# One group of six row turns after the value products, in a score buffer, copied by ScalarE

## Chip, cores and metric

The kernel runs on one core of a Trainium2 chip. The metric is the device time of one execution in microseconds. TensorE (PE in the profile, with its weight loads as PEld), VectorE (DVE), ScalarE (ACT), GpSimd (POOL) and SyncE (SP, which issues most DMAs) each run their own instructions in order and wait for each other by semaphores.

## What is computed

Sigmoid attention over 4 batches and 12 heads of 448 tokens, then a routed layer of 8 experts on the 1,792 tokens, then a dense layer with an ELU curve:

```python
def _attn_ref(q, k, v):
    scores = scale * np.matmul(q, k.transpose(0, 1, 3, 2)) - np.log(S)
    attn = 1.0 / (1.0 + np.exp(-scores))
    return np.matmul(attn, v)
...
x = attn_out.transpose(0, 2, 1, 3).reshape(B * S, H * D)   # 1792 x 768
x = _moe_ref(x=x, **moe_kwargs)     # skip score, argmax over 8 experts, two products, gate
return _moe2_ref(x=x, **moe2_kwargs)  # x @ w_in, ELU, @ w_out
```

## The kernel before

The attention loop runs over 24 steps (`steps`), one for each pair of heads of each batch, six pairs (`hp`) to a batch (`b`), and one more round for the last products. In step n, TensorE makes four groups of scores (`scores`, line 228, six matmuls over two banks each, out of a pool `pss` of three two-bank PSUM buffers), ScalarE turns each group into attention weights with one sigmoid (line 235), and TensorE then makes the sixteen value products of the step before (`mix`, line 242) into the one buffer `po`, which VectorE copies into `xT` (line 250). `xT` holds the attention output with its 768 features on the partitions.

The next stage wants x by token rows in DRAM (`x_d`). So 9 of the 14 tiles of 128 tokens (`LATE`) are turned inside the loop, one in each step with `hp > 1` whose batches lie far enough back. A turned tile is six TensorE transposes (`flip`, line 138), a copy from PSUM into `xr` (line 272) and a store by SyncE (line 274). In the kernel before, `rows` is a generator of two halves. The first half is three transposes behind the score groups and ahead of the value products, into the only buffer of pool `psx`, copied by VectorE; the second half is three transposes behind the value products, into the same buffer, copied by ScalarE. The other five tiles are turned after the loop, two halves each, in buffers of `pss`, and ScalarE makes all ten copies.

Beside this, each step splits half of the next q and k into two parts (`split_qk`: a ScalarE cast on line 220, then a VectorE subtraction on line 221), and VectorE converts 64-bit weights of the last layer by pieces (`narrow`, lines 146 to 166), up to two pieces after each of four points in the step. TensorE, ScalarE and VectorE run in the order of the program text (`manual_schedule`); SyncE's and GpSimd's orders are set by the scheduler. Buffers in a pool go round: a new tile of a tag waits until the readers of the tile that had the buffer are done.

After the loop come the routing of tokens (a chain of small VectorE operations), a gather of rows of `x_d` by GpSimd (line 706), the experts and the dense layer.

Of the kernel before, what the change touches and what calls it, by code (L numbers as in the profile page):

```python
# [12 lines left out]
F32 = mybir.dt.float32  # L13
# [10 lines left out]
P = 128  # L24
B, H, S, D = 4, 12, 448, 64
# [6 lines left out]
KD = DM // P  # L32
# [9 lines left out]
N2 = DM // 2  # L42
# [4 lines left out]
LATE = 9  # L47
# [42 lines left out]
def build(nc, tc, a):  # L90
# [3 lines left out]
    with ExitStack() as top:  # L94
# [42 lines left out]
        def flip(dst, src):  # L137
            nc.tensor.transpose(dst, src, ident)  # L138

        def wide_load(w, i, part=slice(None)):  # L140
            nc.sync.dma_start(w, wide[i].rearrange("p (n t) -> p n t", t=2)[:, part])
# [30 lines left out]
        with ExitStack() as st:  # L172
# [7 lines left out]
            pss = st.enter_context(tc.tile_pool(name="pss", bufs=3, space=PSUM))  # L180
            ps1 = st.enter_context(tc.tile_pool(name="ps1", bufs=1, space=PSUM))
            psx = st.enter_context(tc.tile_pool(name="psx", bufs=1, space=PSUM))
# [17 lines left out]
            xT = xp.tile([P, NP, NT], F32, name="xT")  # L200
            lgT = xp.tile([P, NT], F32, name="lgT")

            def load(b, t, first=False):
                qr = qkp.tile([P, 2, S], F32, name="qr")
                kr = qkp.tile([P, 2, S], F32, name="kr")
                if first:
                    for p in range(2):
                        nc.sync.dma_start(qr[:, p], q[b, t, :, p])
                        (nc.scalar, nc.sync)[p].dma_start(kr[:, p], k[b, t, :, p])
                    return qr, kr  # L210
                nc.sync.dma_start(qr, q[b, t])
                nc.sync.dma_start(kr, k[b, t])
                return qr, kr

            def split_tiles(raw):
                return raw, [qkp.tile([P, 2, S], F32R, name=n) for n in ("qh", "ql", "kh", "kl")]

            def split_qk(which, raw, parts, p=slice(None)):
                r, (hi, lo) = raw[which], parts[2 * which : 2 * which + 2]
                nc.scalar.copy(hi[:, p], r[:, p])  # L220
                nc.vector.tensor_sub(lo[:, p], r[:, p], hi[:, p])

            def scores(at, c, p, qh, ql, kh, kl):
                ps = pss.tile([P, 2, 512], F32, name="ps")
                for i, (kk, qq) in enumerate(((kh, qh), (kh, ql), (kl, qh))):
                    for j in range(2):
                        head = slice(64 * j, 64 * j + 64)
                        nc.tensor.matmul(  # L228
                            ps[:CP, j, :S],
                            kk[head, p, c * CP : (c + 1) * CP],  # L230
                            qq[head, p],
                            start=(i == 0),
                            stop=(i == 2),
                        )
                nc.scalar.activation(  # L235
                    at[:, :, c, :], ps[:CP, :, :S], AF.Sigmoid, bias=bias[:CP], scale=QK_SCALE
                )
# [25 lines left out]
                    )  # L263
                nc.vector.tensor_copy(lgT[:, b * S : (b + 1) * S], lg[:, :S])

            def rows(t, engines, pool=psx, tag="px"):
                xr = rowp.tile([P, DM], F32, name="xr")
                for g in range(2):
                    px = pool.tile([P, 512], F32, name="px", tag=tag)
                    for i in range(3):  # L270
                        flip(px[:, i * P : (i + 1) * P], xT[:, 3 * g + i, t * P : (t + 1) * P])
                    engines[g](xr[:, g * N2 : (g + 1) * N2], px[:, :N2])
                    yield
                nc.sync.dma_start(x_d[t * P : (t + 1) * P, :], xr)

            lgt = xp.tile([P, NTT, E + 1], F32, name="lgt")
# [12 lines left out]
            def run(gen):  # L289
                for _ in gen or ():  # L290
                    pass
# [111 lines left out]
            def load_v(n):  # L403
                vts[n] = qkp.tile([CP, 4, NCH, D], F32, name="vt", bufs=2)
                nc.sync.dma_start(vts[n], v[n // 3, :, 4 * (n % 3) : 4 * (n % 3) + 4])
# [24 lines left out]
            wide_load(wides[0], 0)  # L430
            done_rows = 0
            done_lgt = 0
            row = None
            prev = None
            nxt = None
            for n in range(steps + 1):
                b, hp = divmod(n, NP)
                T, p = divmod(n, 2)
                if p == 0 and n < steps:
                    if n:  # L440
                        cur = nxt
                    if T + 1 < steps // 2:
                        nxt = split_tiles(nxt_raw)
                        if T + 2 < steps // 2:
                            nxt_raw = load(*divmod(T + 2, 3))
                    else:
                        nxt = None
                if p == 1 and T + 1 < steps // 2:
                    load_v(T + 1)
                at = atp.tile([CP, 2, NCH, S], F32, name="at") if n < steps else None  # L450
                po = ps1.tile([P, 512], F32, name="po", tag="po") if n else None
                if m3 is not None and c0 + 1 < n:
                    nc.scalar.copy(wi0[0], m3)
                    nc.vector.tensor_sub(wi0[1], m3, wi0[0])
                    m3 = None
                if conv is None and narrowed < n * 2 * FA // (steps - 1):
                    mf = wi1 if narrowed == 2 else cvp.tile([P, DM], F32, name="mf")
                    w = wides[narrowed % 2]
                    if narrowed + 1 < 2 * FA:
                        wide_load(wides[(narrowed + 1) % 2], narrowed + 1)  # L460
                    sg = cvp.tile([P, DM], I32, name="sg", bufs=1)
                    mg = cvp.tile([P, DM], I32, name="mg", bufs=1)
                    conv = narrow(mf, w, sg, mg, False)
                if row is None and done_rows < LATE and hp > 1 and (done_rows + 1) * P <= b * S:
                    row = rows(done_rows, (nc.vector.tensor_copy, nc.scalar.copy))
                    done_rows += 1
                for c in range(NCH):
                    for c2 in range(NCH):
                        if c == 0 and n < steps:
                            scores(at, c2, p, *cur[1])  # L470
                        if c == 2 and n:
                            mix(c2, n - 1, *prev, po)
                    if nxt and n < steps and c == 1:
                        split_qk(p, *nxt)
                    if row is not None and c in (1, 3):
                        next(row, None)
                    if hp == 1 and b > 0 and c == 0:
                        logits(b - 1)
                    if hp == 1 and b > 0 and c in (2, 3):
                        m = min(4, b * S // P - done_lgt)  # L480
                        if m > 0 and b < B:
                            token_logits(done_lgt, m)
                            done_lgt += m
                    if n > SOON_STEP:
                        next(soon, None)
                    if n > SOON_STEP + 2:
                        next(soon, None)
                    for _ in range(2):
                        if conv is not None and next(conv, 1):
                            if narrowed == 0:  # L490
                                m3, c0 = mf.rearrange("p (c f) -> p c f", c=KD), n
                            elif narrowed != 2:
                                nc.sync.dma_start((wi_d, wo_d)[narrowed % 2][narrowed // 2], mf)
                            narrowed += 1
                            conv = None
                if row is not None:
                    run(row)
                    row = None
                prev = (vts.get(T), at)
            run(soon)  # L500
            logits(B - 1)
# [1 line left out]
            rowp = st.enter_context(  # L503
                tc.tile_pool(name="rowq", bufs=NTT - done_rows, reuse_waits="tile")
            )
            tail_rows = (nc.scalar.copy, nc.scalar.copy)
            run(rows(done_rows, tail_rows, pss, "ps"))
            token_logits(done_lgt, NTT - done_lgt)
            for t in range(done_rows + 1, done_rows + 3):
                run(rows(t, tail_rows, pss, "ps"))  # L510


            choose(SOON, NTT)
# [2 lines left out]
                nc.tensor.matmul(cnt, ones_b, p[:, 0, :E], start=(k_ == 0), stop=(k_ == 1))  # L516
            pos = positions(SOON, NTT, ps1, "po")
            for t in range(done_rows + 3, NTT):
                run(rows(t, tail_rows, pss, "ps"))
            rp = st.enter_context(tc.tile_pool(name="rp", reuse_waits="tile", bufs=1))  # L520

            def rt(shape, name, dt=F32):
# [62 lines left out]
            for k_, p in enumerate(counted):  # L585
                nc.tensor.matmul(
                    ordered, ones_b, p, start=(k_ == 0), stop=(k_ == len(counted) - 1)
# [548 lines left out]
        with ExitStack() as st:  # L1136
# [156 lines left out]
            for s, (bi, f) in enumerate(steps):  # L1293
# [12 lines left out]
                g = curve(nt * P, ph)  # L1306
                if bi + 1 < len(blocks):
                    u0, un = blocks[bi + 1]
                    turn, half = divmod(f - 6, 2)
                    if half == 0 and 0 <= turn < un:  # L1310
                        rows_next = rows_of(u0 + turn)
                    turn, half = divmod(f - 7, 2)
# [47 lines left out]
```

## Time and profile before

| what | us |
|---|---|
| three runs | 937.42, 937.55, 939.18 (median 937.55) |
| the profiled execution | 937.65 |
| its span, first to last instruction | 935.8 |
| TensorE busy in the span | 900.0 (96%) |
| VectorE, ScalarE, GpSimd busy | 560.1, 483.3, 69.0 |
| mean granted TensorE clock | 0.992 |
| attention loop | about 7 to 176 us of the span |

The profiled execution is read as follows. The chain that ended last tells which engine sets the pace at each time; the waits tell for whom an engine stood still; the timeline gives each instruction's start and length. The 1.85 us between span and time lie outside the instructions. A busy TensorE is not one at its peak: matmuls are pipelined, and their ends overlap the next one's start.

### The profile page before, as it was taken

How to read it: one execution, taken by the hardware profiler on the slowest of the kernel's cores; microseconds unless marked ns; L12 is line 12 of the kernel's file. 1: busy time of each engine (PE TensorE's matmuls, PEld its weight loads, DVE VectorE, ACT ScalarE, POOL GpSimd, SP SyncE). 2: the span in 40 equal slices, each digit the busy share in tenths (PEclk: the TensorE clock that was granted, in tenths of full speed). 3: DMA queues.
4: the chain of work that ended last, by engine and by line, in shares of the span. 5: the costliest groups of instructions: out<-in, count | busy, mean ns of one | idle time of the engine just before them, and what ended most of it. 6: DMA issues, size and time to landing. Idle time of an engine off the chain costs nothing.

```text
span 935.8 us, 13725 instructions
## 1 busy us (share of the span) xinstructions
PE 900.0 (96%) x5239; PEld 722.0 (77%) x5239; DVE 560.1 (60%) x871; ACT 483.3 (52%) x681; POOL 69.0 (7%) x69
## 2 busy tenths in 40 slices
PE   9999999899999998898899999999999999999998
PEld 4444444479997997788788888888888888888997
DVE  2776676867564664688488887533443434434664
ACT  7766676443354554576355544544444434443664
POOL 0000000021110110222100000100000100000100
PEclk9999999999999999899999999999999999999999
DMA  8777684499570980991753342100010100000100
GB/s 281 236 245 239 238 285 157 167 349 415 202 284 7 360 297 1 387 369 44 257 186 93 110 119 85 49 20 0 18 35 18 68 1 1 1 1 1 68 1 34
DMA packets 33910, 133.96 MB, mean 143 GB/s; under 512 B 4666, under 2 KB 5818, under 8 KB 33810
## 3 DMA queue, kind: packets, MB, share of 16 engines
q1 hardware_dynamic: 29186, 113.43, 34.5%
q0 software_dynamic: 4480, 19.01, 5.7%
q8 instruction: 57, 0.93, 0.4%
q14 instruction: 43, 0.35, 0.1%
q10 hardware_dynamic: 144, 0.23, 0.1%
HBM read 112.08 MB, written 23.60 MB: 145 GB/s over the span
## 4 chain that ended last, share of the span: by engine, by line
PE 91%; DVE 3%; ACT 3%; issue 2%; DMA 0%; ACTq 0%; DVEq 0%; POOL 0%; POOLq 0%
PE acc L1235 16%; PE pt L1235 10%; PE acc L1202 8%; PE acc L1203 8%; PE acc L1204 8%; PE po L242 6%; PE acc L732 6%; PE acc L733 6%; PE acc L734 6%; PE ps L228 6%; ACT at L235 2%; PE pt L138 1%; PE acc L804 1%; PE acc L138 1%; PE idle L195 1%
## 5 line engine op out<-in xcount | busy, mean ns | idle before, releaser
L725 DVE TENSOR_TENSOR wlo<-raw,whi 128x1536 fp32r<-128x1536 f32 x64 | 111.2, 1756 | 37.5 <-ACT whi L723 36.8
L1211 ACT ACTIVATE m<-acc 128x512 f32<-128x512 f32 (+1 forms) x64 | 35.0, 546 | 173.8 <-PE acc L1204 167.2
L1213 DVE SCALAR_TENSOR_TENSOR m<-m,acc 128x512 f32<-128x512 f32 (+1 forms) x64 | 39.8, 621 | 137.7 <-ACT m L1212 137.7
L723 ACT CAST whi<-raw 128x1536 fp32r<-128x1536 f32 x64 | 94.0, 1481 | 32.7 <-DMA raw<-in_w 9.8
L235 ACT ACTIVATE at<-ps,bias 112x896 f32<-112x896 f32 x96 | 88.9, 1010 | 32.1 <-PE ps L228 32.1
L1235 PE MATMUL acc<-wol,gh 128*128 128x256 f32 x320 | 101.0, 316 | 0.0
L1235 PE MATMUL acc<-woh,gl 128*128 128x256 f32 x320 | 100.5, 314 | 0.0
L1235 PE MATMUL acc<-woh,gh 128*128 128x256 f32 x320 | 100.4, 314 | 0.0
L1203 PE MATMUL acc<-x,wih 128*128 128x512 f32 (+1 forms) x270 | 96.0, 356 | 0.0
L1202 PE MATMUL acc<-x,wih 128*128 128x512 f32 (+1 forms) x270 | 95.9, 355 | 0.0
L1204 PE MATMUL acc<-x,wil 128*128 128x512 f32 (+1 forms) x270 | 95.6, 354 | 0.0
L732 PE MATMUL acc<-whi,both 128*128 128x384 f32 (+1 forms) x236 | 85.6, 363 | 3.3 <-issue 3.3
L733 PE MATMUL acc<-wlo,both 128*128 128x384 f32 (+1 forms) x236 | 84.1, 356 | 0.0
L734 PE MATMUL acc<-whi,both 128*128 128x384 f32 (+1 forms) x236 | 84.0, 356 | 0.0
L242 PE MATMUL po<-at,vt 112*64 112x448 f32 x384 | 77.5, 545 | 0.7 <-DVE xT L250 0.7
L1191 DVE TENSOR_TENSOR wol<-wo,woh 128x768 fp32r<-128x768 f32 x64 | 61.2, 957 | 23.3 <-ACT woh L1190 23.0
L1235 PEld LDWEIGHTS acc<-woh,gh 128*128 128x128 f32 x320 | 60.3, 188 | 10.1
L1235 PEld LDWEIGHTS acc<-wol,gh 128*128 128x128 f32 x320 | 60.3, 188 | 9.3
L1190 ACT CAST woh<-wo 128x768 fp32r<-128x768 f32 x64 | 53.3, 833 | 25.9 <-PE acc L1235 25.8
L1217 DVE TENSOR_TENSOR gl<-m,gh 128x512 fp32r<-128x512 f32 (+1 forms) x64 | 40.1, 626 | 40.5 <-ACT gh L1216 40.5
L1185 DVE TENSOR_TENSOR wil<-wi,wih 128x768 fp32r<-128x768 f32 x60 | 57.4, 956 | 10.9 <-ACT wih L1184 6.0
L1235 PEld LDWEIGHTS acc<-woh,gl 128*128 128x128 f32 x320 | 60.1, 188 | 4.3
(236 smaller groups left out, 1886.9 us busy)
## 6 DMA issues: line engine op xcount, KB each, us to landing
raw<-in_w SPq DMA_DIRECT2D x66, 768.0 KB, 9.8
raw<-in_wi SPq DMA_DIRECT2D x9, 768.0 KB, 7.1
raw<-in_wo SPq DMA_DIRECT2D x9, 768.0 KB, 7.0
vt<-in_v SPq DMA_DIRECT2D x12, 448.0 KB
x_d<-xr SPq DMA_DIRECT2D x14, 384.0 KB, 2.8
raw<-in_wi SPq DMA_DIRECT2D x14, 384.0 KB
raw<-in_wo SPq DMA_DIRECT2D x14, 384.0 KB, 3.1
qr<-in_q SPq DMA_DIRECT2D x11, 448.0 KB, 6.1
```

Source lines behind the costliest of these rows:

```text
L235: nc.scalar.activation(at[:, :, c, :], ps[:CP, :, :S], AF.Sigmoid, bias=bias[:CP], scale=QK_SCALE)
L242: nc.tensor.matmul(po[64 * j : 64 * j + 64, :S], vt[:, 2 * (hp % 2) + j, c, :], at[:, j, c, :], start=(c == 0), stop=(c == NCH - 1),)
L723: nc.scalar.copy(w_hi, raw)
L725: nc.vector.tensor_sub(w_lo, raw, w_hi)
L732: nc.tensor.matmul(o, a_hi, b_hi, start=first, stop=False)
L733: nc.tensor.matmul(o, a_hi, b_lo, start=False, stop=False)
L734: nc.tensor.matmul(o, a_lo, b_hi, start=False, stop=last)
L1191: nc.vector.tensor_sub(pair[1], wo_r[f], pair[0])
L1202: nc.tensor.matmul(o, a, b, start=(cc == 0), stop=False)
L1203: nc.tensor.matmul(o, a, c, start=False, stop=False)
L1204: nc.tensor.matmul(o, wil[:, cc], b, start=False, stop=(cc == KD - 1))
L1235: nc.tensor.matmul(o, a, b, start=(clears and f == 0 and k_ == 0), stop=(f == KF2 - 1 and k_ == 2), skip_group_check=True,)
```

## The change

`rows` is no generator any more. It takes one two-bank buffer of `pss` (the tag of the score groups) for all six transposes, lets ScalarE copy both banks (2 x 384 columns) in one operation, and issues the store. In the loop it is called once, behind the value products; after the loop it is called for the five last tiles.

```diff
-            def rows(t, engines, pool=psx, tag="px"):
+            def rows(t):
                 xr = rowp.tile([P, DM], F32, name="xr")
-                for g in range(2):
-                    px = pool.tile([P, 512], F32, name="px", tag=tag)
-                    for i in range(3):
-                        flip(px[:, i * P : (i + 1) * P], xT[:, 3 * g + i, t * P : (t + 1) * P])
-                    engines[g](xr[:, g * N2 : (g + 1) * N2], px[:, :N2])
-                    yield
+                px = pss.tile([P, 2, 512], F32, name="px", tag="ps")
+                for i in range(KD):
+                    g, o = i // 3, i % 3 * P
+                    flip(px[:, g, o : o + P], xT[:, i, t * P : (t + 1) * P])
+                nc.scalar.copy(xr.rearrange("p (g n) -> p g n", g=2), px[:, :, :N2])
                 nc.sync.dma_start(x_d[t * P : (t + 1) * P, :], xr)
...
-                if row is None and done_rows < LATE and hp > 1 and (done_rows + 1) * P <= b * S:
-                    row = rows(done_rows, (nc.vector.tensor_copy, nc.scalar.copy))
-                    done_rows += 1
+                turn = done_rows < LATE and hp > 1 and (done_rows + 1) * P <= b * S
...
-                    if row is not None and c in (1, 3):
-                        next(row, None)
+                    if turn and c == 3:
+                        rows(done_rows)
+                        done_rows += 1
...
-            tail_rows = (nc.scalar.copy, nc.scalar.copy)
-            run(rows(done_rows, tail_rows, pss, "ps"))
+            rows(done_rows)
             token_logits(done_lgt, NTT - done_lgt)
             for t in range(done_rows + 1, done_rows + 3):
-                run(rows(t, tail_rows, pss, "ps"))
+                rows(t)
```

TensorE in a step of the loop with a tile (`ps` scores, `po` value products, `px` transposes; one of nine such places):

```order
 L228 MATMUL ps<-ql,kh 112x448 x2
 L228 MATMUL ps<-qh,kl 112x448 x2
-L138 MATMUL px<-cst,xT 128x128 x3
 L242 MATMUL po<-at,vt 64x448 x8
-L138 MATMUL px<-cst,xT 128x128 x3
+L138 MATMUL px<-cst,xT 128x128 x6
 L228 MATMUL ps<-qh,kh 112x448 x2
 L228 MATMUL ps<-ql,kh 112x448 x2
```

The three transposes that stood ahead of the value products have joined the three behind them.

VectorE in such a step (`ql` is the subtraction of the q/k split, `mf`, `sg` and `mg` are pieces of the weight conversion):

```order
 L152 TENSOR_SCALAR mg<-raw_105 128x768
 L221 TENSOR_TENSOR ql<-qr,qh 128x896
-L272 COPY xr<-px 128x384
 L154 TENSOR_SCALAR mf<-mg 128x768
 L158 SCALAR_TENSOR_TENSOR sg<-raw_105,sg 128x768
```

The copy of the first half, which stood behind the subtraction, is gone from VectorE.

ScalarE at the last two tiles of the loop and behind it (`at` the sigmoids):

```order
 L220 CAST qh<-qr 128x896
-L272 COPY xr<-px 128x384
+L272 COPY xr<-px 128x768
 L235 ACTIVATE at<-ps,bias 112x2x448 x4
 L220 CAST kh<-kr 128x896
-L272 COPY xr<-px 128x384
+L272 COPY xr<-px 128x768
 L235 ACTIVATE at<-ps,bias 112x2x448 x8
-L272 COPY xr<-px 128x384 x10
-L603 ACT_TABLE_LOAD
-L603 ACTIVATE ex<-dl 128x112
```

The copy keeps its place between a step's cast and the next step's sigmoids and is twice as large; behind the loop five of them stand in the place of ten.

SyncE's DMA issues around the fourth and fifth tile, before:

```order
L274 DMA x_d<-xr 128x768
L212 DMA kr<-in_k 128x896
L274 DMA x_d<-xr 128x768
L141 DMA raw_104<-in_wi 128x1536
L493 DMA wi_d_66<-mf 128x768
L211 DMA qr<-in_q 128x896
```

and in the changed kernel:

```order
L273 DMA x_d<-xr 128x768
L212 DMA kr<-in_k 128x896
L141 DMA raw_104<-in_wi 128x1536
L490 DMA wi_d_66<-mf 128x768
L273 DMA x_d<-xr 128x768
L211 DMA qr<-in_q 128x896
```

A tile's store of rows stands behind a load of raw weights and a store of converted ones (`mf`) there, where it stood ahead of them.

## Rows read from the trace of the kernel before

**Rows 1.** The page's head and its first part: busy time, share of span, instructions.

```profile
span 935.8 us, 13725 instructions
PE 900.0 (96%) x5239; PEld 722.0 (77%) x5239; DVE 560.1 (60%) x871; ACT 483.3 (52%) x681; POOL 69.0 (7%) x69
```

**Rows 2.** Waits of TensorE, 0 to 176 us: waiter, waited for: total us, times, longest.

```profile
PE px L138 <- DVE xr L272: 5.5, 9, 0.6
PE po L242 <- DVE xT L250: 0.7, 1, 0.7
```

**Rows 3.** Chain that ended last, a step with a tile: start us, us, work.

```profile
115.15 2.81 PE ps L228 x24
117.96 0.48 PE px L138 x3
118.43 3.18 PE po L242 x16
121.61 0.56 DVE xr L272
122.22 0.55 PE px L138 x3
122.77 2.81 PE ps L228 x24
```

**Rows 4.** The same chain, a step without a tile.

```profile
130.38 2.82 PE ps L228 x24
133.21 3.16 PE po L242 x16
136.36 2.82 PE ps L228 x21
```

**Rows 5.** Timeline of TensorE, in the loop and behind it: start us, us, work.

```profile
64.16 0.45 PE L228 MATMUL ps<-qh,kh 64*112 64x448 f32 x2
...
65.47 0.37 PE L228 MATMUL ps<-qh,kh 64*112 64x448 f32 x2
...
66.19 0.46 PE L228 MATMUL ps<-qh,kh 64*112 64x448 f32 x2
...
177.65 0.88 PE L138 MATMUL px<-cst,xT 128*128 128x128 f32 x6
178.44 0.66 PE L138 MATMUL pl<-cst,lgT 128*128 128x128 f32 x4
```

**Rows 6.** Timeline of ScalarE around the same step; in brackets idle time before, releaser.

```profile
64.27 0.48 ACT L272 COPY xr<-px 128x384 f32<-128x384 f32 x1 [2.23 <-PE px L138]
65.12 3.70 ACT L235 ACTIVATE at<-ps,bias 112x896 f32<-112x896 f32 x4 [0.38 <-PE ps L228]
68.70 0.95 ACT L220 CAST kh<-kr 128x896 fp32r<-128x896 f32 x1
```

**Rows 7.** Timeline of VectorE there.

```profile
62.07 1.09 DVE L221 TENSOR_TENSOR ql<-qr,qh 128x896 fp32r<-128x896 f32 x1 [1.86 <-ACT qh L220]
63.08 0.55 DVE L272 COPY xr<-px 128x384 f32<-128x384 f32 x1
...
64.88 0.61 DVE L250 COPY xT<-po 128x448 f32<-128x448 f32 x1
```

**Rows 8.** ScalarE's groups by line and shape: busy us, mean ns, idle before.

```profile
L235 ACT ACTIVATE at<-ps,bias 112x896 f32<-112x896 f32 x96 | 88.9, 1010 | 32.1 <-PE ps L228 32.1
L1190 ACT CAST woh<-wo 128x768 fp32r<-128x768 f32 x64 | 53.3, 833 | 25.9 <-PE acc L1235 25.8
```

**Rows 9.** Timeline behind the loop: last row copies, slot numbers, first gather.

```profile
182.59 0.88 ACT L272 COPY xr<-px 128x384 f32<-128x384 f32 x2
...
186.41 0.19 DVE L596 TENSOR_SCALAR slot_tok<-inv 128x28 int32<-128x28 f32 x1 [0.28 <-PE inv L592]
...
187.48 1.18 POOL L706 DMA_INDIRECT xg<-x_d,slot_tok  x1 [7.71 <-DVE gw L608]
```

**Rows 10.** Stretch: us, busy of PE, PEld, DVE, ACT, POOL; clock, DMA share, GB/s.

```profile
380.00:392.00 12.00, 8.71 (x29) 7.64 (x29) 6.18 (x5) 4.32 (x3) 3.97 (x3) 0.72 1.02 408
```

More of the change, by code (lines that the diff above doesn't have):

```diff
@@ L432, in build @@
             done_lgt = 0
-            row = None
             prev = None
@@ L495, in build @@
                             conv = None
-                if row is not None:
-                    run(row)
-                    row = None
                 prev = (vts.get(T), at)
@@ L518, in build @@
             for t in range(done_rows + 3, NTT):
-                run(rows(t, tail_rows, pss, "ps"))
+                rows(t)
             rp = st.enter_context(tc.tile_pool(name="rp", reuse_waits="tile", bufs=1))
```

## The prediction

> **What bounds the kernel now.** I read the busy shares first: TensorE is busy for 900.0 of 935.8 us [rows 1], so an edit matters as far as it shortens or lengthens TensorE's own line. Next the waits of TensorE in the attention stage [rows 2]. The largest is the one that the edit touches: nine times the second half of a tile's transposes stands still for VectorE's copy of the first half, 5.5 us in all. The chain of waits shows it inside one step [rows 3]: the value products start at 118.43 and take 3.18, so TensorE is free at 121.61, VectorE copies until then and 0.56 beyond, and the transposes go on at 122.22. VectorE's timeline says why a copy that was ready before the value products comes so late [rows 7]: it stands in the queue behind the subtraction of the q/k split, and that one had VectorE idle for 1.86 us, until ScalarE's cast was done. So one queue position on VectorE costs TensorE 0.61 us in each of nine steps, and all of it is on the path.
>
> **The steps with a tile.** From one score phase to the next such a step takes 122.77 - 115.15 = 7.62 us [rows 3]; one without a tile takes 136.36 - 130.38 = 5.98 [rows 4]. So a tile costs 1.64 now: the wait of 0.61, and 1.03 for two groups of three transposes (0.48, and 122.77 - 122.22 = 0.55). The edit takes the wait away, since no copy stands between the halves any more: the six write two banks of one buffer. What six in a row cost has a row of its own behind the loop, 178.44 - 177.65 = 0.79 [rows 5], but there other transposes follow. From above, two groups as they are now cost 1.03. Three cost 0.48 where other matmuls follow, and four that stand with others cost less for each, so leaving the transposes for other matmuls costs something once. I take 0.85, nearer to the row of six, since it is the same instruction six times. A tile then costs 0.85, a step with one 6.83, and the gain is 0.79, between 0.61 and 0.85. Nine steps: **7.1 us**, between 5.5 and 7.6.
>
> **What the new copy meets on ScalarE.** I count from the start S of the next score phase (64.16, rows 5). The last transposes end where they did, so the copy starts at S + 0.11 (64.27) [rows 6]. No row shows 768 columns out of two banks. The nearest: 0.48 for 384 columns of one bank [rows 6], 1.01 for 896 columns of two banks with a bias, and 0.83 for 768 columns out of SBUF [rows 8]. On the line between the first two, 768 columns give 0.48 + 384 x (1.01 - 0.48) / 512 = 0.88; I take that, with 0.83 and 1.01 as bounds. It ends at S + 0.99. The first sigmoid started at S + 0.96 [rows 6] after 0.38 of idle time, and four of them take 3.70 where each takes 1.01, so one starts some 0.11 before the end of the one ahead. It can start at S + 0.88, and its scores come at S + 0.96: nothing lost; with a copy of 1.01, 0.05 a step, 0.5 in all. The cover is those 0.38 us of ScalarE.
>
> **What it takes from the score buffers.** The tile takes one of three buffers, so a step with a tile asks five times. The third score group of the next step gets the tile's buffer. It started at S + 1.31 (65.47) [rows 5], the copy is done at S + 0.99, so 0.3 is left. The fourth gets the first group's buffer, as before: it started at S + 2.03 (66.19), just behind the first sigmoid's end at 66.13. The tile itself gets the buffer of its step's second group, whose sigmoid is long done.
>
> **What else moves.** VectorE loses nine copies of 0.55 [rows 7], which it would have had time for; what it gives back is cover for the copy of `po`. That copy started 0.72 after S (64.88) [rows 7], behind subtraction, row copy and two pieces of conversion. The value products now start 0.48 sooner after S, at S + 2.8. In the new step the copy stands 1.09 + 1.4 behind the cast's end (S + 5.49, from rows 6), ends some 8.5 after its own S, and the products need it at 6.83 + 2.8 = 9.6: covered. The cast and subtraction for the next q and k end at about S + 6.6, and the matmuls that read the subtracted part come 0.6 into the next phase, at 7.4: covered by 0.8. Ahead of the loop's end one wait for VectorE is left, 0.7 [rows 2]; it stays. On SyncE three stores of rows go behind a load of raw weights and a store of converted ones; nobody reads them before the gather, and the row buffer is used again two tiles later.
>
> **Behind the loop.** Ten copies become five, on the same transposes; TensorE there follows the routing chain on VectorE, so no gain. The last copy now starts with its sixth transpose, where the last of the two in rows 9 did, some 183.0, and takes 0.88 for 0.48: the last store goes 0.4 later. The gather starts 0.88 after the slot numbers [rows 9], so it may be waiting for that store. Price 0 to 0.4; I take 0.3, since slot numbers alone don't explain its start.
>
> **A rule that speaks against this.** Rows 3 and 6 make the coarser copy harmless, since ScalarE stands idle ahead of the sigmoids and the buffer is free 0.3 early. The Trainium skill says otherwise in general ("Perfetto Trace Analysis", section Optimizing Scalar/DVE Operations): where ScalarE and VectorE are not saturated but leave other engines with gaps, smaller instructions may let work be done sooner. By it the sum would lose what the second rival below loses; the trace agrees only in that ScalarE is at 52% [rows 1], and no run here shows a 768-column copy yet.
>
> **The sum.** 937.65 - 7.1 + 0.3 = 930.9 us. The profiled execution is 0.1 above the median of the runs, which is nothing here.
>
> **Rivals.**
> - *The change doesn't shorten the loop.* Something behind TensorE paces the step: then 936 to 938, with the wait on another row. VectorE is the candidate, as its copy of `po` and its subtraction stand close. Against it: the margins of 0.8 and 1.1 us above, and that steps without a tile run at 5.98 with the same casts and conversions [rows 4].
> - *The copy of two banks is the new bound.* From 0.96 on, each 0.1 us more of it delays the first sigmoid, with it the fourth score group and TensorE, by 0.1 in nine steps. At 1.4 that is 9 x 0.44 = 4.0, so 934.9. From 0.96 + 6.8 / 9 = 1.72 on the kernel is **slower than before**; at 2.0 it is 930.9 + 9.4 = 940.3. For it: two banks and a gap in one operation, no row of just that. Against it: the sigmoid reads two banks with a gap in 1.01 [rows 8].
> - *The clock gives the gain back later.* From 380 to 392 TensorE was busy for 8.71 of 12 us and the granted clock was 0.72 [rows 10], a mixture of the 1.2 and 2.4 GHz levels: 0.28 x 12 = 3.4 us lost. All that follows the loop comes 7 us sooner, and the places where the clock falls may differ. One more such place: 934.3; two: 937.7. Against it: the same waits in the same order, only earlier.
>
> **How the numbers follow.** Forecast 930.9, its own range 929.9 to 932.5: 70%. The loop doesn't follow: 8%. The copy: 10%, of which 3% slower than before. The clock: 12%, mostly one place. A measurement of this kernel can tell about 0.2% (1.9 us) from no change. So faster by more (under 935.7): 70 + 3 + 6 + 8 = 87%; within: 5 + 1 + 3 = 9%; slower: 3 + 1 = 4%. The range must hold 80%: below, 937.55 - 7.6 and half a microsecond of scatter give 929.5; above, it takes in one place of the clock and the half-hidden copy, 935.0.
>
> **What would show it.** In the changed kernel the wait of transposes for VectorE's `xr` is gone; steps with a tile take 6.7 to 7.0; ScalarE's copy lasts 0.83 to 1.01 and the first sigmoid starts within 1.05 of S; the third score group starts at S + 1.3, not later; the last value products end some 7 us earlier. Wrong would be a new wait of `ps` for ScalarE's `xr`, of `po` for `xT` in the nine steps, or a gather more than 0.5 later after the slot numbers.

## The result and the profile after

The changed kernel takes 930.88 us (median of 6 runs, 926.99 to 933.67). The kernel before, run beside it, takes 938.21 (6 runs, 937.42 to 940.47). The ratio is 0.9916 with a 95% interval of 0.9891 to 0.9941: 7.3 us or 0.8% faster. The forecast was 930.9.

The page's head of the profiled execution (926.99 us), to be set beside [rows 1]:

```profile
span 925.2 us, 13707 instructions
PE 894.3 (97%) x5239; PEld 719.4 (78%) x5239; DVE 556.0 (60%) x862; ACT 485.6 (52%) x676; POOL 72.3 (8%) x69
```

TensorE does the same 5239 matmuls in 5.7 us less busy time, and the span is 10.6 shorter. The nine VectorE copies of the loop are gone (871 to 862), and ScalarE has five copies fewer.

The profiled execution is the quickest of its six, so I split the two spans at three marks of the chain: the first score matmul, the last logits (line 256), and the first expert product (line 725, in the kernel before line 732).

| us | to the first scores | loop | tail to the first expert product | all behind it | span |
|---|---|---|---|---|---|
| before | 7.30 | 168.75 | 22.44 | 737.31 | 935.8 |
| after | 6.46 | 161.33 | 22.96 | 734.45 | 925.2 |
| difference | -0.84 | -7.42 | +0.52 | -2.86 | -10.6 |

The loop's 7.42 is what the edit does. The first and last columns differ as much between executions of kernels that are the same there (a second profile of the changed kernel has 737.24 in the last; the kernel before with some spare copies has 6.43 in the first), so the medians, 7.3 apart, hold no more than the loop.

The waits of TensorE from 0 to 172 us, to be set beside [rows 2] (waiter, waited for: total us, times, longest):

```profile
PE idle L195 <- POOL zero_b L189: 1.0, 1, 1.0
PE ps L228 <- ACT at L235: 0.9, 1, 0.9
PE po L242 <- DVE xT L250: 0.7, 1, 0.7
```

These are all that the view lists: the nine waits of `px` for VectorE's `xr` are gone, no wait for ScalarE's `xr` has come, and the one for `xT` ahead of the loop's end stayed as it was.

The chain that ended last, a step with a tile (beside [rows 3]):

```profile
62.58 2.82 PE ps L228 x24
65.40 3.16 PE po L242 x16
68.56 0.80 PE px L138 x6
69.36 2.82 PE ps L228 x24
```

A step with a tile now takes 69.36 - 62.58 = 6.78 us, where it took 7.62. Scores and value products are what they were; six transposes stand in one group of 0.80.

ScalarE's timeline in the step that starts at 62.51 (beside [rows 6]; in brackets the idle time before and its releaser), its group of row copies (beside [rows 8]), TensorE's timeline and VectorE's (beside [rows 5, 7]):

```profile
62.62 0.80 ACT L272 COPY xr<-px 128x768 f32<-128x768 f32 x1 [1.41 <-PE px L138]
63.48 3.70 ACT L235 ACTIVATE at<-ps,bias 112x896 f32<-112x896 f32 x4
```

```profile
L272 ACT COPY xr<-px 128x768 f32<-128x768 f32 x14 | 11.0, 803 | 21.9 <-PE px L138 17.6 <-issue 4.3
```

```profile
62.51 0.46 PE L228 MATMUL ps<-qh,kh 64*112 64x448 f32 x2
...
63.83 0.36 PE L228 MATMUL ps<-qh,kh 64*112 64x448 f32 x2
...
64.54 0.46 PE L228 MATMUL ps<-qh,kh 64*112 64x448 f32 x2
...
65.33 3.23 PE L242 MATMUL po<-at,vt 112*64 112x448 f32 x16
```

```profile
63.58 0.62 DVE L250 COPY xT<-po 128x448 f32<-128x448 f32 x1
```

With S = 62.51, the copy starts at S + 0.11, lasts 0.80 and ends at S + 0.91. The first sigmoid starts at S + 0.97 (S + 0.96 before), with no idle time ahead of it any more: the cover of 0.38 us that ScalarE had is used up but for some hundredths. The third score group starts at S + 1.32 (1.31 before), the fourth at S + 2.03 (the same). VectorE's copy of `po` ends at 64.20, 1.13 before the value products.

### The profile page after: what moved, and what is told of

The parts are those of the page before. It is cut to its first block, busy times and chain, and to the rows that moved or that the text cites. A ratio compares the mean times of both kernels' runs of the same rounds, so it can differ in the third digit from the quotient of the medians.

```text
span 925.2 us, 13707 instructions
## 1 busy us (share of the span) xinstructions
PE 894.3 (97%) x5239; PEld 719.4 (78%) x5239; DVE 556.0 (60%) x862; ACT 485.6 (52%) x676; POOL 72.3 (8%) x69
## 4 chain that ended last, share of the span: by engine, by line
PE 94%; DVE 2%; issue 1%; ACT 1%; DMA 1%; POOL 0%; ACTq 0%; DVEq 0%; POOLq 0%
PE acc L1228 16%; PE pt L1228 10%; PE acc L1195 8%; PE acc L1196 8%; PE acc L1197 8%; PE po L242 8%; PE ps L228 7%; PE acc L725 6%; PE acc L726 6%; PE acc L727 6%; PE pt L138 1%; PE acc L797 1%; PE acc L138 1%; PE acc L798 1%; PE px L138 1%
## 5 line engine op out<-in xcount | busy, mean ns | idle before, releaser
L725 PE MATMUL acc<-whi,both 128*128 128x384 f32 (+1 forms) x236 | 84.4, 357 | 3.4 <-issue 3.4
L727 PE MATMUL acc<-whi,both 128*128 128x384 f32 (+1 forms) x236 | 83.1, 352 | 0.0
```

Source lines behind the costliest of these rows:

```text
L725: nc.tensor.matmul(o, a_hi, b_hi, start=first, stop=False)
L727: nc.tensor.matmul(o, a_lo, b_hi, start=False, stop=last)
```

## The experiments

Twelve kernels ran. The stages of all of them, by the same three marks (the profiled execution of each), with median and ratio to the kernel before, measured on the same chip:

| kernel | first scores | loop | tail | behind it | median us | ratio, 95% |
|---|---|---|---|---|---|---|
| two copies of 384 a tile | 6.31 | 161.28 | 23.31 | 745.4 | 936.45 | 0.9987 (0.9964 to 1.001) |
| transposes in two groups, one copy | 6.62 | 163.60 | 23.62 | 735.16 | 933.4 | 0.9949 (0.993 to 0.9967) |
| before, first half copied by ScalarE | 6.13 | 162.66 | 23.71 | 734.3 | 931.44 | 0.993 (0.9905 to 0.9955) |
| loop of after, tail of before | 6.19 | 161.93 | 24.20 | 742.58 | 936.83 | 0.9991 (0.9967 to 1.0016) |
| the copy made twice | 5.83 | 167.26 | 29.81 | 742.6 | 948.73 | 1.0085 (1.0053 to 1.0117) |
| after, unchanged, again | 6.27 | 161.28 | 23.41 | 737.24 | 930.69 | 0.9886 (0.9857 to 0.9914) |
| after, 14 spare ScalarE copies | 6.40 | 161.38 | 24.02 | 735.9 | 929.59 | 0.9878 (0.9849 to 0.9908) |
| before, 14 spare ScalarE copies | 6.43 | 169.10 | 25.00 | 737.97 | 940.23 | 0.9988 (0.9964 to 1.0012) |
| two copies in the loop only | 6.37 | 161.23 | 23.22 | 746.58 | 937.4 | 0.9964 (0.994 to 0.9989) |
| two copies, 14 spare copies | 6.46 | 161.25 | 23.76 | 741.83 | 937.84 | 0.9985 (0.9967 to 1.0003) |
| after, TensorE's code shifted | 5.92 | 161.25 | 23.80 | 741.93 | 934.07 | 0.9951 (0.9928 to 0.9975) |
| two copies, TensorE's code shifted | 5.76 | 161.41 | 24.23 | 738.5 | 929.12 | 0.9902 (0.9866 to 0.9938) |

The first five tell the parts of the change apart; the other seven follow up what stands in the column behind the tail.

**The place in VectorE's queue alone.** The kernel before, with ScalarE for the first half as well:

```diff
-                    row = rows(done_rows, (nc.vector.tensor_copy, nc.scalar.copy))
+                    row = rows(done_rows, (nc.scalar.copy, nc.scalar.copy))
```

> The kernel before with one word changed: the first half of a tile is copied by ScalarE and not by VectorE; the halves stay apart and share their one buffer. Theory (the wait was the place in VectorE's queue, behind the subtraction that waits for the cast): ScalarE's copy stands right behind the cast and is done some 0.5 us before the value products end, so the wait of 0.61 goes, a step with a tile takes 7.0 us and the loop is 5.5 us shorter than before, 2.1 longer than in the changed kernel. Rival (one buffer for two halves is what makes the wait): the wait stays, on ScalarE, and the loop is as long as before.

The chain of a step with a tile, and ScalarE's copy of the first half in it:

```profile
62.37 2.83 PE ps L228 x22
65.20 0.48 PE px L138 x3
65.68 3.16 PE po L242 x16
68.84 0.48 PE px L138 x3
69.31 2.84 PE ps L228 x21
```

```profile
66.84 0.95 ACT L220 CAST kh<-kr 128x896 fp32r<-128x896 f32 x1
67.67 0.50 ACT L272 COPY xr<-px 128x384 f32<-128x384 f32 x1
```

The copy stands right behind the cast and ends at 68.17, 0.67 before the value products do. No wait is left between the halves. The step takes 69.31 - 62.37 = 6.94, so 0.68 of the 7.62 are gone: the wait of 0.61, and 0.07 because the second three no longer start from a standstill (0.48 where it was 0.55). The loop is 6.09 us shorter than before. One word in the program gives 6.1 of the loop's 7.4, and the ratio to the kernel before (0.993) lies inside the changed kernel's interval. No run left the copy on VectorE and put it ahead of the subtraction; that the place decides, and not the engine, is read from the two traces: VectorE's copy takes 0.55 [rows 7] and ScalarE's 0.50, but VectorE's starts only as the value products end.

**The joining alone.** The changed kernel with three transposes ahead of the value products and three behind, in one two-bank buffer, and one copy:

```diff
                     flip(px[:, g, o : o + P], xT[:, i, t * P : (t + 1) * P])
+                    if i == 2:
+                        yield
...
-                    if turn and c == 3:
-                        rows(done_rows)
+                    if turn and c == 1:
+                        row = rows(done_rows)
                         done_rows += 1
+                        next(row)
+                    if turn and c == 3:
+                        run(row)
```

> The changed kernel, but the first three transposes of a tile stand ahead of the value products again, as in the kernel before, in the first bank of the same score buffer; the other three and the one copy stay behind them. No copy stands between the halves. Theory: the wait of 0.61 us stays away, but two groups of three cost 1.03 us where one of six costs 0.80, so a step with a tile takes 7.0 us and the loop is 2.1 us longer than in the changed kernel, up to 3.0 where the first half also waits for the second sigmoid of its step. Rival (the whole gain is the removed wait): the loop is as long as in the changed kernel.

```profile
62.97 2.82 PE ps L228 x22
65.79 0.04 issue
65.83 0.55 PE px L138 x3
66.38 3.16 PE po L242 x16
69.54 0.48 PE px L138 x3
70.01 2.81 PE ps L228 x22
```

A tile costs 0.04 + 0.55 + 0.48 = 1.07 in this chain, against 0.80 for six in one group. Nine times 0.27 is 2.4; the loop is 2.27 longer than that of the changed kernel. Joining is worth about a quarter of a microsecond a step, measured from the changed kernel; measured from the run above, whose halves stand apart in one bank each, the step goes from 6.94 to 6.78, which is 0.16. The two gains share something, so 6.09 and 2.27 are not to be added.

**One copy or two.** The changed kernel with a copy for each bank:

```diff
-                nc.scalar.copy(xr.rearrange("p (g n) -> p g n", g=2), px[:, :, :N2])
+                for g in range(2):
+                    nc.scalar.copy(xr[:, g * N2 : (g + 1) * N2], px[:, g, :N2])
```

> The changed kernel, but ScalarE copies the two banks of a tile in two operations of 384 columns each, one for each bank, behind each other. Theory (the gain comes from TensorE's line: no wait, one group of six): the loop is as long as in the changed kernel, 6.78 us for a step with a tile, within 0.1; two copies take about 0.38 + 0.48 = 0.86 for 0.80, and the first may start half a group earlier. Rival (the coarse copy costs something, finer ones let the next work start sooner): steps with a tile get shorter by up to 0.4 us, the loop by up to 3.6.

```profile
62.43 0.86 ACT L273 COPY xr<-px 128x384 f32<-128x384 f32 x2 [1.41 <-PE px L138]
63.30 3.70 ACT L235 ACTIVATE at<-ps,bias 112x896 f32<-112x896 f32 x4
```

Two copies take 0.86 together, one takes 0.80, and with S = 62.33 the first sigmoid starts at S + 0.97 either way. The loop is the same to 0.05 us. Yet the kernel takes 936.45, and its stage behind the tail 745.4: 936.45 - 930.88 = 5.6 us that the copies' own stage doesn't show. More on them below.

The Trainium skill's rule that the prediction weighed ("Perfetto Trace Analysis", section Optimizing Scalar/DVE Operations) speaks for the smaller pieces where a copy leaves another engine with gaps. Here the one copy gives TensorE no wait, so that condition isn't met, and the two loops, 161.28 and 161.33, show no gain from smaller pieces.

**The copy twice as long.** ScalarE makes each tile's copy a second time:

```diff
                 nc.scalar.copy(xr.rearrange("p (g n) -> p g n", g=2), px[:, :, :N2])
+                nc.scalar.copy(xr.rearrange("p (g n) -> p g n", g=2), px[:, :, :N2])
```

> The changed kernel with ScalarE's copy of a tile made twice, so that it holds ScalarE for 1.50 us (two behind each other) and not 0.80. Theory (ScalarE sets the first sigmoid, and the fourth score group waits for that one's buffer; the copy has no cover left, since in the changed kernel no idle time stands between copy and first sigmoid): the first sigmoid starts 0.70 later, the fourth score group and with it TensorE wait 0.6 to 0.7 in each of nine steps, steps with a tile take 7.4 us, the loop is 5.4 to 6.3 us longer than in the changed kernel, and TensorE's waits for the sigmoid at the fourth group grow by that. Rival (only the tile's own buffer matters, asked for by the third group 0.3 after the copy's end): 0.4 in each step, 3.6 in all. Second rival (there is cover elsewhere): under 1 us in all.

The waits of TensorE from 0 to 174 us, its third score group, and ScalarE, in a step with S = 61.87:

```profile
PE ps L228 <- ACT xr L273: 2.9, 9, 0.3
```

```profile
63.66 0.46 PE L228 MATMUL ps<-qh,kh 64*112 64x448 f32 x2 [0.32 <-ACT xr L273]
```

```profile
61.97 0.80 ACT L272 COPY xr<-px 128x768 f32<-128x768 f32 x1 [1.40 <-PE px L138]
62.81 0.80 ACT L273 COPY xr<-px 128x768 f32<-128x768 f32 x1
63.50 3.71 ACT L235 ACTIVATE at<-ps,bias 112x896 f32<-112x896 f32 x4
```

The first sigmoid starts at S + 1.63, 0.66 later, and the third score group waits for the tile's buffer nine times. A step takes 69.33 - 61.87 = 7.46, 0.68 more, and the loop 5.93 more. This is the price that the second rival named: past its cover, the copy costs TensorE what it is longer. The median is 18 us above the changed kernel's, and 12 of that lie behind the loop: in the tail, which has a wait of 4.2 for gathered rows where the changed kernel has one of 0.3, and in the stage behind it.

**The tail.** The loop of the changed kernel, with the five last tiles in two halves and ten copies as before:

```diff
+            def late_rows(t):
+                xr = rowp.tile([P, DM], F32, name="xr")
+                for g in range(2):
+                    px = pss.tile([P, 512], F32, name="px", tag="ps")
...
+                    nc.scalar.copy(xr[:, g * N2 : (g + 1) * N2], px[:, :N2])
...
-            rows(done_rows)
+            late_rows(done_rows)
```

> The changed kernel, but the five tiles behind the loop are turned and copied in two halves each, ten copies, as in the kernel before; the loop is as changed. Theory (the larger last copy sends the last store 0.4 us later, the rows that the experts read arrive later): the way from the last logits to the first expert product is 22.5 us again, as in the kernel before, and not 23.0. Rival (that half microsecond is scatter of the gather's DMA): it lies anywhere between 22.5 and 23.1.

The tail took 24.20, not less than 22.96. The tail of the kernel before is 22.44 in one profile and 25.00 in another (with spare copies at the start), that of the changed kernel 22.96 and 23.41. The coarser copies can't be seen in this. And again the stage behind is longer (742.58).

**What costs 5 us behind the loop.** By now one thing was unexplained: kernels with the same loop differ by up to 12 us behind the tail (734.45 and 746.58). The page's instruction queue and TensorE's waits without a visible cause lead there. In the kernel with two copies the chain has one wait of more than a microsecond that the changed kernel hasn't, and from 399.70 to 403.16, while it lasts, the DMA view shows a packet of an instruction queue (second fence: queue, packets, MB, share):

```profile
399.53 0.17 PE acc L728
399.70 3.46 issue
403.16 0.45 PE acc L726
```

```profile
q8 instruction: 1, 0.02, 2.0%
```

The first guess was that ScalarE's number of instructions sets where code stands. Fourteen one-column copies ahead of the first cast shift it, in the changed kernel and in the one before:

```diff
+            spare = xp.tile([P, 14], F32, name="spare")
+            for i in range(14):
+                nc.scalar.copy(spare[:, i : i + 1], bias)
```

> The changed kernel with 14 copies of one column more on ScalarE, ahead of its first cast, where it stands idle for 1.5 us waiting for q. They do nothing for the result and take no time on the path; ScalarE's program is 14 instructions longer, as with 14 tiles copied in two operations each. Theory (the place of the code behind the loop makes the extra wait in the expert stage that the kernel with two copies for a tile showed, and not its loop): the wait of TensorE of 2.5 to 3.5 us near 400 us is there, the time is 4 to 7 us above the changed kernel's. Rival (that wait comes from the two copies or the runs' scatter): same as the changed kernel, 931 within 1.5.

> The kernel before with the same 14 spare copies ahead of ScalarE's first cast. If the place of the code makes the extra wait whatever the loop, this is 4 to 7 us above the kernel before; if not, the same within 1.5 us. The loop is as in the kernel before, 168.7 us, either way.

> The changed kernel once more, unchanged. Theory (the loop is the same in each execution, and what differs from run to run is the granted clock behind the loop): loop within 0.3 us of 161.3 us, run times between 926 and 934, longer ones with a lower mean clock. Rival: the loop itself scatters by microseconds.

The times did not move: 929.59 beside 930.69 for the unchanged one, and 940.23 beside 939.79 for the kernel before. The loop of the unchanged one was the same again (161.28). Two more runs put the two copies into the loop alone, and the spare copies beside the two copies.

> The changed kernel with two copies of 384 columns for each of the nine tiles in the loop, and one copy of 768 for the five tiles behind it. Two copies everywhere took 936.4 with the loop as short as in the changed kernel and one more unexplained TensorE wait at about 400 us, with a lower clock beside it. Theory: what costs the 5.5 us lies in the later stage and depends on the count of ScalarE's instructions, so nine more cost the same as fourteen more; loop 161.3, total 935 to 938, the extra wait of 2 to 3.5 us there. Rival: the later stage depends on the tail's copies (two copies in the tail alone also had the extra wait), so that this kernel is like the changed one: 930 to 932, no extra wait near 400 us.

> Two copies of 384 for all fourteen tiles, and fourteen copies of one column by ScalarE ahead of the first cast. If the extra wait at about 400 us hangs on where ScalarE's later instructions stand in its program, the spare ones move it: the wait is gone or elsewhere, total 930 to 932 with the loop still at 161.3. If two copies cost the time by what they do (their stores, their buffers), the fourteen spare copies change nothing: 935 to 938, with the extra wait in the same place.

Both keep a wait there (3.38 and 1.63) and take 937.4 and 937.84. So nine more copies suffice, and ScalarE's position has no part in it that these runs show: the kernel with 14 spare copies and the one with ScalarE for both halves have as many ScalarE instructions as the one with two copies, and not the wait. The last guess was TensorE's own code. Nine of the fifteen warm-up matmuls at the start were cut into 36 short ones, the same columns:

```diff
+                for _ in range(short):
+                    nc.tensor.matmul(ps[:, 0], zero_b[:, 0], zero_b[:, 0], start=True, stop=True)
...
-            keep_warm(15)
+            keep_warm(6, 36)
```

> Two copies of 384 for all fourteen tiles (936.4 before, with an extra wait of 3.5 us near 403), with the same shift of TensorE's code by 27 more short matmuls at the start. Theory (TensorE waits for its own code): the extra wait near 403 is gone or has moved, and the stage behind the loop is another than 745. If it goes and no other comes, the total is 930 to 932. Rival (something that the two copies do sets the wait): it stays at about 403 with 2 to 3.5 us, total 936 to 938.

> The changed kernel, with nine of TensorE's fifteen warm-up matmuls of 512 columns at the start cut into 36 of 128: the same columns, 27 more matmuls with their weight loads, so that all of TensorE's later code stands further back by those. Theory: the waits of 3 us and more in the expert stage, in which a packet of the instruction queue arrives, are TensorE waiting for its own code, and where they fall hangs on where its code stands at the branches. Then the pattern of the waits (1.8 at 230, 3.4 at 376, 3.9 at 449) changes: one more, one less or one elsewhere, and the stage behind the loop takes some 2 to 8 us more or less than the changed kernel's 734 to 737. Rival: TensorE's code has no part in it. Then the pattern stays, and the total is that of the changed kernel, 930 to 932, but for the start, which may be up to 1 us later.

With this shift, the kernel with two copies takes 929.12, where it took 936.45: the ratios to the kernel before, 0.9902 and 0.9987, have intervals that don't touch. The stretch from 398 to 412 us, first with two copies, then with the shift too (us, busy of PE, PEld, DVE, ACT, POOL; clock, DMA share, GB/s):

```profile
398.00:412.00 14.00, 10.54 (x44) 9.13 (x43) 8.93 (x7) 6.30 (x6) 1.33 (x2) 0.88 0.88 341
```

```profile
398.00:412.00 14.00, 14.00 (x72) 12.31 (x71) 12.43 (x11) 10.81 (x9) 3.18 (x3) 1.00 1.01 393
```

TensorE stood still for 3.46 of the 14 us, and was granted 0.88 of its clock, 0.12 x 14 = 1.7 more (0.71 from 403.16, where it went on, to 409, a mixture of the levels 1.2 and 2.4 GHz); with the shift it is busy throughout at full clock. These 5.1 us are about what two copies cost in the medians (5.6), and half of what the last column of the two profiles differs by (10.95). In the changed kernel the same shift does the opposite: a wait of 1.20 comes up in the same place, the stage behind the tail takes 741.93, and the median is 934.07. (Its interval overlaps with that of the changed kernel's first runs, not with that of the second.)

```profile
402.60 0.45 PE L727 MATMUL acc<-whi,both 128*128 128x384 f32 x1 [1.20 <-issue]
```

What TensorE does there is in the traces too. Its sequencer (PEldq in the views) stands at a branch, `tc.If(k > 1)` of the routing (line 1100 of the changed kernel). The length of that branch, in ns, and its start, in the changed kernel, with two copies, with two copies and the shift, and in the changed kernel with the shift:

```profile
L1100 PEldq COMPARE_BRANCH  x1: 460/460/460, 393.6 to 393.6; - x1
```

```profile
L1101 PEldq COMPARE_BRANCH  x1: 6275/6275/6275, 396.8 to 396.8; - x1
```

```profile
L1103 PEldq COMPARE_BRANCH  x1: 457/457/457, 398.2 to 398.2; - x1
```

```profile
L1102 PEldq COMPARE_BRANCH  x1: 4002/4002/4002, 398.5 to 398.5; - x1
```

With two copies the branch lasts from 396.83 to 403.11, and the first matmul behind the wait starts at 403.16; matmuls that were issued ahead of the branch run until 399.70. The fourteen profiles (before, after and the twelve above) fall into two groups by it. In eight it takes 0.36 to 0.50, in the six with the extra wait 4.0 to 6.3. From the transposes ahead of it (391.19 in the changed kernel, 394.42 with two copies) to the next ones it is 20.63 to 20.67 in the eight and 22.10 to 25.95 in the six; and a packet of the instruction queue starts within 0.4 behind those transposes in the eight, 3.9 to 6.1 behind them in the six.

So the place of TensorE's code decides on this wait, and not what the copies do. Why a second copy for each tile moves that place shows on TensorE as well: its score groups (line 228) have nine semaphore instructions more, one in each step with a tile. In the changed kernel and with two copies:

```profile
L228 PEldq EVENT_SEMAPHORE  x8: 51/51/51, 13.7 to 147.5; - x8
```

```profile
L228 PEldq EVENT_SEMAPHORE  x17: 51/51/51, 13.5 to 151.3; - x17
```

With two copies the program has 25 instructions more: the 14 copies, these nine, and two of the same kind elsewhere on TensorE. In the twelve profiles without the shift, TensorE's sequencer has 141 or 142 instructions of its own where the extra wait is absent and 146 to 152 where it is there; the fourteen spare ScalarE copies leave them at 141 in the changed kernel. The 27 more matmuls of the shift turn both cases round (152 without the wait, 141 with it).

What stays open is the rest of the last column. In the shifted changed kernel the stretch around the wait is 1.5 longer than in the changed one, of 4.7 to 7.5 in the whole stage; the other slow branches and the clock differ by one to three microseconds from profile to profile. Executions of one kernel scatter as well: 931.57 to 939.17 with two copies in the loop only, 929.27 to 938.28 in the shifted changed kernel, the short ones at a mean granted clock of 0.995 or 0.996, the longest at 0.987 and 0.985.

## Why the prediction was right

**The wait that goes.** 0.61 in each of nine steps, as the first part said; its row is gone, and the one-word experiment bears out that the place behind the subtraction in VectorE's queue was its cause. One reading was off: it is the subtraction that runs until the value products end (120.60 to 121.69 in that step of the kernel before); the copy starts at 121.61.

**The six transposes.** 0.80 in the chain, for 0.85 taken between 0.79 and 1.03. The row of six behind the loop [rows 5] was the right neighbour. (That four cost less for each than three holds for the busy times, 0.66 and 0.55; the 0.48 that the prediction set beside them leaves out what overlaps with the next matmul.) A step takes 6.78 for 6.83, and the loop gained 7.42 for 7.1 (5.5 to 7.6).

**The new copy.** 0.80 for 0.88, just under the lower bound of 0.83, so this sign missed, on the harmless side. The line through 384 and 896 columns went through a row with a bias and a sigmoid; the row nearest to it was the 768 columns out of SBUF. The sigmoids start at S + 0.97 as said, and the slope past 0.96 was shown by the copy made twice: there copy and repeat end at S + 1.74, 0.78 beyond it, and a step was 0.68 longer, where the rival's price is 0.1 for each 0.1.

**The score buffers.** The third group had 0.4 to spare for 0.3, the fourth started at S + 2.03 as before. VectorE's copy of `po` ended 1.13 before the products, for 1.1.

**The tail: wrong in mechanism, its size luck.** The step took 0.3 because the gather might wait for the last row store. In this kernel it doesn't. Slot numbers and first gather of the changed kernel (beside [rows 9]), and the first matmuls that wait for what it brings:

```profile
178.16 0.18 DVE L589 TENSOR_SCALAR slot_tok<-inv 128x28 int32<-128x28 f32 x1 [0.28 <-PE inv L585]
...
179.22 1.17 POOL L699 DMA_INDIRECT xg<-x_d,slot_tok  x1 [7.71 <-DVE gw L601]
...
187.45 0.99 PE L138 MATMUL pt<-cst,xg 128*128 128x128 f32 x7 [0.30 <-DMA xg<-x_d,slot_tok]
```

The gather starts 179.22 - 178.34 = 0.88 after the slot numbers, and 179.22 - 167.79 = 11.43 after the last logits; before it was 187.48 - 186.60 = 0.88 and 187.48 - 176.05 = 11.43. The tail is 0.52 longer in this pair of profiles, but tails of unchanged code differ by more (22.44 and 25.00), so the term should have been 0 with a scatter of up to 2.6 microseconds. The wait that the prediction feared does seem to come once the stores are late enough: with the copy made twice the last store is issued at 183.4 and not at 175.4, and the gather starts at 190.37, 6.73 after the slot numbers (183.64). That it waits for the stores there is not shown; the view names no releaser.

**The clock.** The third rival, one more place of lowered clock, didn't come true for this kernel: its own wait of 3.4 at 372 to 375.5 passed at full clock in the profiled execution, where the kernel before had 0.72 [rows 10], and at 0.68 in the second profile of the same kernel.

```profile
372.00:384.00 12.00, 8.60 (x40) 7.25 (x40) 7.90 (x6) 6.29 (x5) 4.21 (x3) 1.00 1.01 405
```

```profile
370.00:380.00 10.00, 5.80 (x23) 5.48 (x22) 5.29 (x4) 2.52 (x2) 3.35 (x3) 0.68 1.00 410
```

But the argument against it, that the same waits come in the same order, only earlier, was weak. Of the nine profiles with a loop of 161.2 to 162, five have one wait more behind it, and those kernels took 3 to 7 us more in the median. What such a place costs begins, by the runs above, with a slow branch of TensorE's; the clock comes on top. The forecast held because this program has none of them more than the one before, and that was luck: the prediction looked at the clock and at the order of the waits, not at TensorE's branches, and the kernel with two copies, whose loop is as short, took 936.45, above the range.

**The total.** That the median (930.88) meets the forecast (930.9) so closely is luck too. The six runs lie between 926.99 and 933.67, the loop gained 0.3 more than forecast, and the 0.3 of the tail stood for a wait that this kernel hasn't.

## What to carry to other kernels

When a busy engine waits for a short copy, look in the copy's queue first: moving it to an engine that stands idle just then gave 6.1 of the 7.4 us, and joining the transposes the rest; one copy or two made no difference to the loop. Compare the stage that was edited, between two marks in the trace, and not only the total. Where an edit costs or gains some microseconds in a stage that it doesn't touch, look at the lengths of the busy engine's branches there, and shift the code by something neutral before the edit gets the blame or the credit.

## What the runs showed of the hardware

TensorE waits up to 4.2 us at some places of the expert and dense stages, with nothing that it waits for in the view of waits. The three largest in the changed kernel (ending at 229.85, 375.52 and 449.20) have their counterparts in the kernel before (237.87, 383.44, 459.71); the first stands in an arm of a branch (line 1084). Each ends just as a slow branch of TensorE's does: of its 35 branches in the changed kernel 29 take under 0.5 us, and those that end at 229.79, 375.46 and 449.14 take 5.08, 6.03 and 5.94. In six that were looked at in four kernels and the changed one, each of 3 us or more, a packet of instruction queue q8 came in during the wait, beside other transfers at 334 to 417 GB/s in all; at the three shorter extra waits (2.45, 1.63 and 1.20) it came 0.2 to 1.4 us ahead. One packet says little by itself, since the changed kernel has 31 of them between 170 and 500 us; what tells is when it comes. In the kernel with two copies the 18 us ahead of the extra wait hold no such packet; in the changed kernel the corresponding stretch, 379 to 396.5, holds one:

```profile
q1 hardware_dynamic: 1094, 5.97, 82.8%
q0 software_dynamic: 320, 1.20, 18.0%
q8 instruction: 1, 0.02, 0.4%
```

That TensorE stands at a branch is seen in the traces; that the branch stands for its code is read from these packets and from the shift. The shifted changed kernel fits this: it has no packet from 383 to 400, one at 400.05, and the wait of 1.20 that ends at 402.60.

The Trainium skill describes such a wait ("Runtime: NRT & Kernel Launch", section Instruction fetch mechanics): code comes in blocks over a DMA queue of the sequencer's own, mostly hidden, but a taken branch out of the blocks at hand stalls until its block has come. The trace agrees in the branch (6.28 us with two copies, 0.46 without), in the packets and in the effect of the shift; the price here, 3.46 us and 1.7 by the clock behind it, is this case's own.

All fourteen profiles fall into the same two groups by the stage behind the tail: 734.3 to 738.5 where no such wait was added, 741.8 to 746.6 where one was. The means of the groups, 736.4 and 743.5, are 7.1 apart, nearly as much as the edit gained.
